# Attention through packed queries with a maxout layer: projection 1 moved to other PSUM banks, and a new order of the steady list

## The chip, the cores and the metric

One core of a Trainium2 chip. The metric is the device time of one execution in microseconds; the kernel is one launch, and the host only lays out inputs and outputs. Several runs are made and their median is told; the profile is of one execution of its own.

## The reference

Eight batches of eight heads, 576 positions and 64 numbers a head; 32 packed queries `p` per head; then a layer with 512 inputs, 768 hidden units and 512 outputs. All in fp32.

```python
p_packed = sm_attn(p, k, v)              # 32 packed queries attend over 576 keys
out = sm_attn(q, p_packed, p_packed)     # 576 queries attend over the 32 packed rows
x = out.transpose(0, 2, 1, 3).reshape(B * S, H * D)
h = np.maximum(np.maximum(x @ w1, x @ w2), x @ w3)
return h @ w_out
```

## The kernel before, in words

The second attention and the first layer are joined: `project` (line 444) computes p_packed @ w for each of six tiles j of 128 hidden units, all three weight matrices at once, and the layer is then the attention weights times that product. Each fp32 operand of a large product is split into a high and a low part, and three matmuls stand for one.

Work goes by batch, and each batch has steps with a letter: S scores of the packed queries (`scores`, line 263), A their maximum and exponential (`weigh`, line 281), X the turning of the exponentials, two transposes on DVE and then 16 small copies issued on SyncE (`spread`, line 325), V the packed values (`values`, line 344), K their turn into `pt_sb`, Q the second scores (`queries`, line 376), B the second softmax (`attend`, line 394), P the projection, N the first layer of one tile (`layer_in_fast`, line 535, from batch 2 on), E the maximum over its products (`maximum_fast`, line 579), H splits and differences of the hidden units (`halves`), T differences of the attention weights, O the output layer (`layer_out_fast`, line 771) and F its end with the stores. Small k, v, q and w are loads on SyncE's queue.

The order is written out by hand, in three lists of words: START (batches 0 and 1 and the weights), LOOP (run for batches 2 to 6) and LAST (batch 7). In a word the letter is the step, the first digit the batch, counted from the loop's own, and the next ones the tile, group or half; v, g or a at the end put it on DVE, POOL or ACT. Each time a word comes up, that step's generator goes on to its next `yield`. So N05 is the next piece of tile 5 of this batch, and P11 the next piece of projection 1 of the next batch; v11 loads v of group 1 of the next batch. On each engine and on SyncE's queue instructions stand in the order of the words. A word for a batch beyond the last is passed over.

In the loop PE works through tiles 0 to 5 of batch b and its output layer, and between them the small steps of batch b+1: scores, values, queries and projections 0 to 2. Projections 3 to 5 of a batch come in its own turn. The small steps use a part of the TensorE array (64*32 or 128*32 in the profile), the tiles and the output layer the whole (128*128).

PSUM has two pools: `ps_big` (two buffers of two banks: scores, values, queries, projections 0, 1, 2 and 5) and `ps_moe` (four banks: the sums of tiles and output layer, and projections 3 and 4). Where a projection lies in `ps_moe`, its r = 0 and r = 1 are two tiles, and each is read by instructions of its own; in `ps_big` one instruction reads both. The readers are ACT (`pf` line 469, `ph` line 475) and DVE (`pl` line 477). A tile's sums are e, x, u, y and f, a bank each; DVE's joins (line 587) and ACT's copies read them. In SBUF the pool with tag "b" has eight buffers, shared by the loads of k, q and v, the two sides of the 16 copies, and the hidden units.

`values` takes its matmuls so that groups 0 and 1 alternate: two matmuls read v of group 0, the next two of group 1. The last 16 of 80 read the small part of v that the second DMA of `load_v` (line 181) brings.

Of the kernel before, what the change touches and what calls it, by code (L numbers as in the profile page):

```python
# [64 lines left out]
E100 B21 E101 C65 W0a E111 E100 P12 N11 C62 C62 C63 C63 P13 C62 P12 W0v H03a C64 N05 C63 E101 N05 P13 E051a  # L65
C63 P12 B21 C62 N05 E111 B20 P15 E051 E051 C64 W0g P14 P15 P15 N13 N13 B21g B21 H02g H03v H03v N12 C64 E120a
N12 E120 E130a E130 N13 N15 N13 N13 E130 R0v H05a N15 N13 H03v N15 N15 N12 N12 C64 W2v N15 W1v W2v E131a E131
N12 N12 E150a E150 N15 E131 E150 H10v B21 W1g W2g W0a W0g W2a W2v E151a W1g E151 E121a W1a E120 W1v W2a H05v
H05g P14 H05g O0 O0 E121 E121 P14 E151 H03a W2g W1a W1v N14 N14 H01a F0 F0 H03v N14 N14 N14 W1v N14 W2v R3v
R1v P21 O0 E140a O0 W2v W1a E141a B21a F0 H05a H11g R2g B21 E140 E140 E141 E141 H01v H14v H12v B20v H12a H05v  # L70
O0 F0 F0 O0 O0 O0 H12g O0 B20 B20 B20a F0 W1v H11v H10a H10v H11v H11g W2v O0 B20 F0 F0 H13a k31 P21 P21 P21
F0 P21g F0 O0 B20g B20 O0 O0 O0 B21v B21 F0 B20a P22 F0 P21v F0 P20 F0 F0 F0 H14a H14g B21a H13v H13v P21v
H15a P20 H13v O1 O1 O1 O1 H15v H15v O1 H11a H11v P21a H13a H15v F1 F1 F1 P22 P22 H13v k30 P21v H15a H15v O1 O1
O1 O1 O1 B20v O1 O1 F1 F1 F1 P20 F1 O1 T2g T2v B21v T2v O1 T2g F1 F1 T2a P20 P20g F1 R5v F1 F1 P22 F1 F1 F1
# [825 lines left out]
```

## Time and profile before

| | us |
|---|---|
| median of 3 runs (457.0 to 457.44) | 457.03 |
| the profiled execution, its own time | 456.87 |
| its span, first to last instruction | 454.8 |
| PE busy | 448.5 |
| VectorE (DVE) busy | 389.0 |
| GpSimd (POOL) busy | 266.7 |
| ScalarE (ACT) busy | 253.7 |

The span is what the profile shows; the time of an execution holds some 2 us more around it. PE's busy time is a union of matmuls whose ends are modelled, so two starts are the safer measure of what a matmul costs. An engine's idle time counts only where PE waits for it.

### The profile page before, as it was taken

The page shows a single profiled execution, that of the slowest core. Times are in us where ns is not written, and L with a number is a line of the kernel's source. Part 1 is how long each engine was busy: PE and PEld are TensorE (multiplying, and loading weights), DVE is VectorE, ACT ScalarE, POOL GpSimd, SP SyncE. Part 2 cuts the span into 40 slices and gives each one's busy share as a digit, 9 for nine tenths or more (in the row PEclk, how much of TensorE's full clock was granted, in tenths as well). Part 3 has the DMA queues.
Part 4 walks back from the last instruction along what each step waited for, and adds up shares of the span by engine and source line. Part 5 has one row for each costly group of instructions (what it writes and reads, how often), then busy time and mean ns, then how long its engine had stood idle before and what let it go on. Part 6 is the DMA issues. An engine that isn't in the chain of part 4 may idle for free.

```text
span 454.8 us, 11856 instructions
## 1 busy us (share of the span) xinstructions
PE 448.5 (99%) x4616; PEld 391.0 (86%) x4616; DVE 389.0 (86%) x825; ACT 253.7 (56%) x552; POOL 266.7 (59%) x280
## 2 busy tenths in 40 slices
...
GB/s 315 398 386 370 330 66 275 2 0 1 140 109 169 111 178 1 61 208 90 128 0 134 161 144 48 27 203 81 175 1 79 192 95 4 1 105 1 1 2 104
DMA packets 35783, 55.68 MB, mean 122 GB/s; under 512 B 17296, under 2 KB 26512, under 8 KB 35728
## 3 DMA queue, kind: packets, MB, share of 16 engines
...
q14 instruction: 19, 0.16, 0.1%
...
## 4 chain that ended last, share of the span: by engine, by line
PE 82%; DMA 12%; SPq 3%; DVE 1%; ACT 1%; issue 1%; POOL 0%; POOLq 0%; DVEq 0%; ACTq 0%
PE mo L784 22%; PE mx L543 10%; PE me L543 9%; PE mo L707 7%; DMA wi<-in_wi 7%; PE mu L543 6%; PE pw L459 6%; PE mf L543 6%; PE mi L630 6%; PE my L543 3%; DMA q<-in_qt 3%; SPq L339 2%; DMA v<-in_va 2%; PE s L386 2%; PE av L357 2%; PE s L273 1%
## 5 line engine op out<-in xcount | busy, mean ns | idle before, releaser
L672 POOL TENSOR_TENSOR r<-r 128x288 f32<-128x288 f32 (+1 forms) x39 | 45.4, 1164 | 59.1 <-DVE r L672 22.9
L477 DVE SCALAR_TENSOR_TENSOR pl<-pw,ph 128x768 fp32r<-128x768 f32 (+1 forms) x61 | 46.7, 775 | 11.4 <-ACT ph L475 11.2
L486 POOL TENSOR_TENSOR pf<-pf 128x128 f32<-128x128 f32 x72 | 40.7, 576 | 10.1 <-ACT pf L469 6.8
L153 POOL TENSOR_TENSOR sl<-pf,sh 128x384 fp32r<-128x384 f32 x28 | 30.6, 1100 | 27.2 <-DVE sh L150 17.7
L630 PE MATMUL mi<-a2h,ph 128*128 128x288 f32 x144 | 44.1, 306 | 0.0
L630 PE MATMUL mi<-a2l,ph 128*128 128x288 f32 x144 | 42.5, 295 | 0.0
L630 PE MATMUL mi<-a2h,pl 128*128 128x288 f32 x144 | 42.4, 294 | 0.0
L475 ACT ACTIVATE ph<-pw 128x768 fp32r<-128x768 f32 (+1 forms) x61 | 40.0, 680 | 2.8 <-PE pw L459 1.9
L459 PE MATMUL pw<-w_sb,pt 64*32 64x384 f32 x768 | 39.1, 490 | 0.1
L469 ACT ACTIVATE pf<-pw 128x512 f32<-128x512 f32 (+1 forms) x48 | 22.3, 492 | 26.4 <-PE pw L459 26.3
L225 POOL TENSOR_TENSOR w_sb<-w_sb,wi 128x512 int32<-128x512 int32 x18 | 23.7, 1327 | 21.7 <-DVE w_sb L221 16.2
L543 PE MATMUL me<-a2h,ph 128*128 128x288 f32 x108 | 32.6, 302 | 0.0
L630 PEld LDWEIGHTS mi<-a2h,ph 128*128 128x128 f32 x144 | 27.0, 188 | 6.4 <-issue 3.0
L784 PE MATMUL mo<-ych,xh 128*128 128x288 f32 x108 | 32.1, 298 | 0.0
L784 PE MATMUL mo<-ych,xl 128*128 128x288 f32 x108 | 31.9, 295 | 0.0
L543 PE MATMUL me<-a2h,pl 128*128 128x288 f32 x108 | 31.8, 294 | 0.0
L543 PE MATMUL me<-a2l,ph 128*128 128x288 f32 x108 | 31.8, 294 | 0.0
L784 PE MATMUL mo<-ycl,xh 128*128 128x288 f32 x108 | 31.8, 294 | 0.0
L148 ACT COPY r<-me 128x288 f32<-128x288 f32 x35 | 14.2, 405 | 25.1 <-PE me L543 25.1
L630 PEld LDWEIGHTS mi<-a2l,ph 128*128 128x128 f32 x144 | 27.0, 188 | 0.1
L630 PEld LDWEIGHTS mi<-a2h,pl 128*128 128x128 f32 x144 | 27.0, 188 | 0.0
L648 DVE TENSOR_TENSOR r<-mi,r 128x288 f32<-128x288 f32 x48 | 20.6, 447 | 3.1 <-PE mi L630 2.0
...
## 6 DMA issues: line engine op xcount, KB each, us to landing
...
q<-in_qt SPq DMA_DIRECT2D x16, 576.0 KB, 6.2
wi<-in_wi SPq DMA_DIRECT2D x18, 512.0 KB, 8.4
v<-in_va SPq DMA_DIRECT2D x16, 512.0 KB, 7.3
wi<-in_wo SPq DMA_DIRECT2D x6, 512.0 KB, 6.0
...
```

Source lines behind the costliest of these rows:

```text
L153: on(default).tensor_tensor(out=lo, in0=src, in1=hi.bitcast(F32), op=ALU.subtract)
L225: nc.gpsimd.tensor_tensor(out=dst.bitcast(I32), in0=dst.bitcast(I32), in1=up, op=ALU.add)
L459: nc.tensor.matmul(out=ps[r][NP * n:NP * n + NP, 0:NW * P], lhsT=pt_sb[b % 2][o, NP * n:NP * n + NP], rhs=w_sb[o, j, n * NW * P:(n + 1) * ...
L469: nc.scalar.activation(out=f[:, r], in_=x[:, :, 0:2 * P], func=AF.Copy, scale=2.0 ** -WS)
L475: nc.scalar.activation(out=hi[:, r], in_=x, func=AF.Copy, scale=2.0 ** -WS)
L477: nc.vector.scalar_tensor_tensor(out=lo[:, r], in0=x, scalar=2.0 ** -WS, in1=hi[:, r].bitcast(F32), op0=ALU.mult, op1=ALU.subtract,)
L486: on("g").tensor_tensor(out=f[:, k], in0=f[:, x], in1=f[:, y], op=op)
L543: nc.tensor.matmul(out=ps[:, 0:HS], lhsT=w[wi], rhs=x[xi], start=first and n == 0, stop=n == 2, skip_group_check=not first,)
L630: nc.tensor.matmul(out=sums[b, j, hf, x][:, 0:HS], lhsT=w[:, r, x * P:(x + 1) * P], rhs=a[:, c], start=(r == 0 and n == 0), stop=(r == R - ...
L672: less = lambda out, x, y: on("g").tensor_tensor(out=out, in0=x, in1=y, op=ALU.subtract)
L707: nc.tensor.matmul(out=ps[:, 0:HS], lhsT=w[:, x, m * P:(m + 1) * P], rhs=h[:, z], start=(p == 0 and i == 0), stop=(p == NQ - 1 and i == 2),)
L784: nc.tensor.matmul(out=ps[:, 0:HS], lhsT=w[:, x, m * P:(m + 1) * P], rhs=h[:, z], start=(not onto and p == 0 and i == 0), stop=(p == NQ - ...
```

## The change

Projection 1 joins 3 and 4 in `ps_moe` from batch 2 on, with two tiles and two sets of reads. The list LOOP is written anew, START from the end of its twelfth line, and LAST too. In LOOP, PE's order changes in these places: scores stand ahead of tile 0 instead of behind its first product; the two projections 3 and 5 come after tile 0 instead of after tile 1; queries come one product later; and projections 0, 2 and 1 stand together ahead of the last two products of tile 5, where 0 and 2 stood behind its first product and 1 behind its last. SyncE's order in LOOP was v11, q11, v10, the copies X1, q10, k20, k21; it is now q11, k20, v10, the copies X1, v11, q10, k21. In START behind the copies it was w64, w65, q21, q20, w62, w63, k31, k30; it is now w62, w65, w64, q20, w63, q21, k30, k31. Many small steps change engine or place. The lines below are LOOP in full, the first changed lines of START, the last of LAST, and the function.

```diff
 START = """
 ...
-C51 P04 E031a N04 N04 N04 P05 E031 B11 v20 B11a E040v E040 B10 H01a H01v N04 N04 N04 E021 w61 C61 E031 P05
-E041a P05 N05 N05 N05 E040 w60 C60 B10g B10g B11g H00a N10 C61 E041 P11 Z20 E050a H00v X2 C60 C60 E041 C61
-E050 P11 V201 Z21 V201 N11 N11 K2 w64 N10 C61 E110v E110 E050 H01g H01g w65 C65 C65 N11 q21 N11 N10 K2a E100v
-N10 H04v H04a q20 Q2 N11 w62 N10 E111a E110 C60 W0v N10 W0v W0v W0a w63 W0g H02v H02a E101a C65 P13 H04v B20
+C51 P04 E031a N04 N04 N04 P05 E031 B11 v20 B11a E040v E040 B10 H01a H01v N04 N04 N04 E021 w61 E031 H00a H00g
+Z20 P05 w60 C60 P05 N05 E041a E041 N05 E041 C61 C61 B10g B10v H01v P11 B11g N10 E050a H02v E040 H04g N10 N10
+C60 X2 Z21 H04a H02a V201 P11 N05 C60 H04v E100a C61 C61 E100 C60 E050 E050 w62 C62 N05 N05 E051a E051 N10 N10
+w65 C65 E101a W0v W0g W0g R1v N11 w64 q20 V201 K2 K2a C65 C65 N11 N11 E110a E101 N11 w63 H03a H02v E110 E110
+C65 H03v E100 W0a q21 C63 Q2 B20 B21 N11 N11 E111v E111 E111 W0g W0a C63 C63 P13 P15 C64 P13 P13 H03v C64 N10
 ...
 LOOP = """
-N00 S1 A11 N00 N00 N00 A10 E00a E00a E00a N00 N00 E00 E00a E00 N00 N00 N00 v11 E00 E00 E00 A10 Z10 E00 A11 A11
-X1 X1 N01 N01 N01 E01a E01a N01 N01 N01 E01a E01 E01a N01 N01 q11 E01 E01 E01 E01 N01 E01 H01v H00g H00g H00g
-P03 P03 P03 P03 P03 P03 P03 P05 v10 N02 H01v H01g N02 N02 N02 P05 E02a E02a N02 E02a N02 N02 P03v E02 E02a
-H01g N03 N02 N02 E02 E02 P03g P03v P03a P03g N03 N03 Z11 E02 E02 E02 E03a E03a H02v N03 N03 E03a N03 H01g E03
-E03a N03 N03 E03 P05 X1 P05 E03 P04 H02g H02g V101 P04 N03 P04 P04 P04 q10 V101 P04 P04 K1 K1v N04 E04a N04
-P05g E03 E03 E03 P04g P05g P04g Q1 P04g k20 E04a N04 B10 E04a P04g P04g H03a N04 N04 H01g N04 N04 V101 B10
-B10g E04 E04a N05 E05a N04 N04 P10 B11 E04 A10 E04 P05v P12 N05 N05 E04 E04 B10 B10 P05g P10 E04 P05g P05 B11
-P10 N05 P10 P10g E05a N05 E05a E05 E05a N05 E05 H04g H04a N05 E05 N05 N05 B11g H03v P11 H04v O0 O0 P12 P12 B11
-O0 P10g E05 E05 F0 H03v E05 B11 O0 B10a B10 B10v H05a B11a H05v P11 P11 H03g P05 P05 F0 F0 k21 H03a H05v O0 F0
-P12 B10 H03v O0 O0 H05g H05a B11 F0 P10g P11 H05v F0 O0 O0 O0 B11g B11 P10a P11g B10a B10g T1g F0 F0 F0 O0
-B11a F0 P12g B11v F0 O0 P12v O0 F0 P12g T1g T1v T1v P11v P11v P10v O0 T1a T1v P11v P11g P11 P12a F0 T1a T1v F0
-P12g P12 P10 P10 P11 P11 P10 P12 P12
+S1 A11 q11 k20 A10 N00 N00 N00 E00a v10 E00a E00v A10 N00 E00 N00 N00 X1 E00a E00 N00 E00 N00 N00 A11 P03 P05
+P03 P03 X1 E00 E00 N01 E00 P03 P03 P03 P03 P03g P03v H00g H00v N01 N01 N01 H00g E01a E01a E01v N01 E01 N01 X1
+E01a N01 N01 N01 E01 N02 N02 N02 E01 P05 E01 E01 E01 E02a E02a A11 Z10 P03g E02a N02 N02 N02 N02 H01g E02 E02a
+N02 E02 E02 P05 E02 E02 H01g H01g v11 N03 E03v P03a N02 E02 N03 N03 P03g E03a E03a N03 N03 H01g N03 N03 P05
+E03 E03a P05v P05g E03 N03 P04 V101 P05v H02v E03 E03 E03 Z11 N03 P05g P04 P04 P04 P04 P04 P04 V101 V101 N04
+P04g P04g K1 H02a N04 N04 K1a P04g P04a q10 H02v E04v E04a E03 Q1 P05g B10 B10 P04g N04 E04a H01a E04 N04 N04
+N04 E04a E04 N04 N04 N05 E05a E04 H01g N05 N05 N05 E04 E05a E05a H03a A10 N05 N05 N05 E04 E04 B11 B10g B10
+H04g H04g E05 P10 P12 B11 E05a P11 N05 H04v B11g P11 P12 P11 P11 P05 P12 E05 E05 N05 E05 B10 B10a O0 O0 O0 O0
+E05 E05 F0 P11 B10 P11 P12 P11 P12v H05a H03g H03g H05v P10 H03v B11 F0 F0 H05g F0 B11 B11a B11 O0 O0 O0 H03a
+P11g B10v B10 k21 F0 P10 F0 P11v P11g H03v O0 H05g H05a H05v O0 O0 P05 P12g P12g F0 F0 P05 F0 P10 P10g B10a
+B10g B11g F0 B11 B11a P12a P10g O0 O0 T1g F0 O0 P10v P10g T1v F0 B11v T1v P11a T1v T1a T1v P10v T1a T1g P10
+P11g F0 P10 O0 P10 F0 P12g P12 P12 P12
 """
 ...
 LAST = """
 ...
-E04 N04 H02a E04 E04 E04 P05g P05a N05 N05 P05g N05 N05 E05v E05v E05a E05 N05 N05 E05v H04g H04a H04v N05 E05
-E05 H03a N05 E05 H02g O0 N05 E05 E05 H05a O0 O0 O0 F0 F0 F0 H05v H05v H01g H01v F0 H03g O0 H03g P05 H03v H01v
-H03a H03v H05v H05v F0 O0 O0 P05 P05 F0 F0 O0 H05v O0 F0 F0 O0 F0 O0 O0 F0 O0 F0 F0 O0 F0
+P05a E04 E04 E04 E04 H02a N04 E04 P05g P05 H04v N05 E05a H02v N05 N05 N05 E05a N05 E05a N05 N05 E05 E05a N05
+N05 H04g E05 E05 E05 E05 E05 H05v H05v H03g H04g H05v H03v O0 O0 O0 H01g H01a H05v H03g F0 F0 F0 O0 F0 O0 F0
+O0 F0 H03v H03g H01v P05 P05 H03v H05a H05v O0 O0 F0 F0 O0 F0 O0 F0 O0 O0 F0 O0 F0 O0 F0 F0
 """
 ...
     def project(b, j):
 
         parts = [slice(0, R)]
-        if j == 0 and b == 0 or j in (3, 4) and b >= 2:
+        if j == 0 and b == 0 or j in (1, 3, 4) and b >= 2:
 
             parts = [slice(r, r + 1) for r in range(R)]
             ps = [ps_moe.tile([P, 512], F32, name=f"pw{b}_{j}_{r}", tag="moe") for r in range(R)]
 ...
```

## Rows read from the trace of the kernel before

**Rows 1.** The page of the profile, busy time of each engine (share of the span) and its instructions.

```profile
PE 448.5 (99%) x4616; PEld 391.0 (86%) x4616; DVE 389.0 (86%) x825; ACT 253.7 (56%) x552; POOL 266.7 (59%) x280
```

**Rows 2.** Busy time by windows, one steady batch: the stretch, its length and, for each engine, busy us and instructions; then the granted clock of TensorE as a share of full speed, DMA share and GB/s.

```profile
246.80:299.80 53.00, 53.00 (x567) 47.02 (x567) 47.11 (x100) 29.77 (x68) 33.69 (x37) 1.00 0.35 104
```

**Rows 3.** The timeline of PE around the projections 0 and 2 of the next batch, which are one block (start in us, us from the first start to the last end, engine, line, operation, out<-in, tile, count).

```profile
276.21 0.29 PE L543 MATMUL mf<-a2h,pl 128*128 128x288 f32 x1
276.34 0.29 PE L543 MATMUL mf<-a2l,ph 128*128 128x288 f32 x1
276.56 1.52 PE L459 MATMUL pw<-w_sb,pt 64*32 64x384 f32 x32
278.01 0.40 PE L543 MATMUL mx<-a2h,ph 128*128 128x288 f32 x1
278.25 0.29 PE L543 MATMUL mx<-a2h,pl 128*128 128x288 f32 x1
```

**Rows 4.** The timeline of PE around projection 1 of the next batch, between tile 5 and the output layer; the same columns.

```profile
281.57 0.29 PE L543 MATMUL mf<-a2l,ph 128*128 128x288 f32 x1
281.80 0.88 PE L459 MATMUL pw<-w_sb,pt 64*32 64x384 f32 x16
282.60 0.40 PE L784 MATMUL mo<-yah,xh 128*128 128x288 f32 x1
282.84 0.30 PE L784 MATMUL mo<-yah,xl 128*128 128x288 f32 x1
```

**Rows 5.** The timeline of PE in the same batch: its first matmul, scores, values and queries of the next batch.

```profile
246.62 0.29 PE L543 MATMUL me<-a2h,ph 128*128 128x288 f32 x1
...
247.51 0.47 PE L273 MATMUL s<-kt 64*32 64x288 f32 x8
...
267.46 1.46 PE L357 MATMUL av<-v,xt 128*32 128x64 f32 x80
...
271.15 0.47 PE L386 MATMUL s<-q,pt 64*32 64x288 f32 x8
```

**Rows 6.** The timeline of SyncE's queue in that batch (start, us from the first issue to the end of the last, line, tile, count of DMAs).

```profile
247.73 0.41 SPq L184 DMA_DIRECT2D v<-in_va  x1
...
248.81 0.53 SPq L193 DMA_DIRECT2D q<-in_qt  x1
249.43 0.38 SPq L184 DMA_DIRECT2D v<-in_va  x1
...
254.73 10.87 SPq L339 DMA_DIRECT2D xt<-x  x16
265.70 0.54 SPq L193 DMA_DIRECT2D q<-in_qt  x1
```

**Rows 7.** The DMA issues of two narrow windows that hold the first v load of a batch (195.0 to 195.5 and 247.5 to 248.15): count, KB each, us from issue to landing.

```profile
v<-in_va SPq DMA_DIRECT2D x1, 512.0 KB, 3.9
...
v<-in_va SPq DMA_DIRECT2D x1, 512.0 KB, 4.5
```

**Rows 8.** The same view of windows that hold the q load behind the 16 copies: 159.5 to 161, 213.25 to 214 and 265.65 to 267 (318.5 to 320 and 371.8 to 373 have the row of the third again).

```profile
q<-in_qt SPq DMA_DIRECT2D x1, 576.0 KB, 5.7
...
q<-in_qt SPq DMA_DIRECT2D x1, 576.0 KB, 3.6
...
q<-in_qt SPq DMA_DIRECT2D x1, 576.0 KB, 4.2
```

**Rows 9.** The timeline of DVE at the start of that batch: maximum and negated scaled maximum, then joins of tile 0, then the two transposes that SyncE copies (in brackets the idle time before, and what ended it).

```profile
248.87 0.76 DVE L286 TENSOR_REDUCE mx<-s 128x1 f32<-128x576 f32 x1 [0.62 <-PE s L273]
...
250.52 0.15 DVE L287 TENSOR_SCALAR nm<-mx 128x1 f32<-128x1 f32 x1
250.60 0.46 DVE L587 TENSOR_TENSOR r<-my,r 128x288 f32<-128x288 f32 x1
250.97 0.45 DVE L587 TENSOR_TENSOR r<-me,r 128x288 f32<-128x288 f32 x1
...
253.24 1.43 DVE L333 STREAM_TRANSPOSE x<-a 128x576 f32<-128x576 f32 x2
```

**Rows 10.** The timeline of ACT there: the exponential of r = 0.

```profile
250.83 0.75 ACT L291 ACTIVATE a<-s,nm 128x576 f32<-128x576 f32 x1
```

**Rows 11.** The timeline of PE in the first list: the places where it is idle between 66 and 76 us.

```profile
67.21 1.44 PE L357 MATMUL av<-v,xt 128*32 128x64 f32 x74 [0.15 <-DMA xt<-x]
...
75.55 0.72 PE L386 MATMUL s<-q,pt 64*32 64x288 f32 x16 [1.03 <-DMA q<-in_qt]
```

**Rows 12.** The timeline of SyncE's queue there.

```profile
65.94 1.01 SPq L172 DMA_DIRECT2D wi<-in_wo  x2
68.68 1.31 SPq L193 DMA_DIRECT2D q<-in_qt  x2
70.04 2.03 SPq L172 DMA_DIRECT2D wi<-in_wo  x2
```

**Rows 13.** Groups of instructions by line and shape, 194 us to the end, DVE (count, busy us, mean ns of one, idle before).

```profile
L477 DVE SCALAR_TENSOR_TENSOR pl<-pw,ph 128x768 fp32r<-128x768 f32 x17 | 15.9, 938 | 3.5 <-ACT ph L475 3.5
...
L477 DVE SCALAR_TENSOR_TENSOR pl<-pw,ph 128x384 fp32r<-128x384 f32 x20 | 10.5, 552 | 5.8 <-ACT ph L475 5.8
```

**Rows 14.** The timeline of DVE around the end of tile 5 in that batch: a wide split, and the reading of tile 5's x.

```profile
281.15 0.75 DVE L153 TENSOR_TENSOR ybl<-r,ybh 128x576 fp32r<-128x576 f32 x1
...
282.85 0.45 DVE L587 TENSOR_TENSOR r<-mx,r 128x288 f32<-128x288 f32 x1
```

More of the change, by code (lines that the diff above doesn't have):

```diff
@@ L65 @@
[L65 to L74, printed above, removed]
@@ L75 @@
-P20v P20v P20a T2v T2a P21 T2g P22g P22g P22g P22g P22g P20v P20 P22 P20 R4g P20 F1
+C51 P04 E031a N04 N04 N04 P05 E031 B11 v20 B11a E040v E040 B10 H01a H01v N04 N04 N04 E021 w61 E031 H00a H00g
+Z20 P05 w60 C60 P05 N05 E041a E041 N05 E041 C61 C61 B10g B10v H01v P11 B11g N10 E050a H02v E040 H04g N10 N10
+C60 X2 Z21 H04a H02a V201 P11 N05 C60 H04v E100a C61 C61 E100 C60 E050 E050 w62 C62 N05 N05 E051a E051 N10 N10
+w65 C65 E101a W0v W0g W0g R1v N11 w64 q20 V201 K2 K2a C65 C65 N11 N11 E110a E101 N11 w63 H03a H02v E110 E110
@@ new lines @@
+C65 H03v E100 W0a q21 C63 Q2 B20 B21 N11 N11 E111v E111 E111 W0g W0a C63 C63 P13 P15 C64 P13 P13 H03v C64 N10
+C62 C62 N05 C64 P15 W0g P15 N13 N13 N13 H01v P12 W0g W0a C62 B21 P14 C63 E130a E051 P12 B21g N13 N13 N15 N15
+E150a E101 E130 H01a P12 N12 W1g k30 C64 H10v N12 N12 W2g W2g E131v E131 E120a H03v W1g W1v E130 W2v E120 E120
+W1a E150 N13 E131 H05a N12 N15 N15 W1v H05v H05g W2a W2v W2a H05g W0g E150 P14 P14 N12 N12 E121a E151a O0 N15
+N14 N14 E121 E121 E151 B21 B21 B21v H01g B21 H03a B20 E140a N14 N14 N14 F0 W1a E140 E140 W2v W2v R2g O0 F0 W1v
@@ new lines @@
+O0 O0 E141a B21v H05a B20v B20 H03v H12v W1v F0 F0 H05v W2a H10a W1a W1g N14 E141 E141 N15 E151 H13g O0 F0 O0
+O0 O0 O0 O0 O0 H11a H12a H12v H10v W2v k31 F0 R0v O0 O0 F0 F0 F0 H13v H14g H14a H13g H13v F0 O0 H11v H11g R3g
+P22 P22 B20 B20v P20 B20 H11v F0 F0 F0 F0 H11a F0 F0 H14v B20v B21 H15a O1 O1 H13a H15v H15g H15v O1 O1 F1 P20
+P20 O1 O1 H11v B20 H15a H15v H13v O1 P22 P22 P20 P20g P22g P22g F1 B21a F1 F1 F1 F1 F1 O1 O1 O1 F1 F1 R4g B20a
+B20g T2g T2g P21 B21v T2v T2g T2a T2v O1 F1 F1 P20v P20g P21 P21 P21 P21 P21 P21 P21v P22v F1 F1 O1 O1 F1 P20a
@@ L76 @@
+P20v P20 T2a O1 P21g P21g P21a T2g R5g P22a P22g F1 P21g F1 P20 P20 P22
 """
 LOOP = """
-N00 S1 A11 N00 N00 N00 A10 E00a E00a E00a N00 N00 E00 E00a E00 N00 N00 N00 v11 E00 E00 E00 A10 Z10 E00 A11 A11
-X1 X1 N01 N01 N01 E01a E01a N01 N01 N01 E01a E01 E01a N01 N01 q11 E01 E01 E01 E01 N01 E01 H01v H00g H00g H00g
-P03 P03 P03 P03 P03 P03 P03 P05 v10 N02 H01v H01g N02 N02 N02 P05 E02a E02a N02 E02a N02 N02 P03v E02 E02a
-H01g N03 N02 N02 E02 E02 P03g P03v P03a P03g N03 N03 Z11 E02 E02 E02 E03a E03a H02v N03 N03 E03a N03 H01g E03
@@ L98 @@
-N02 N02 N02 E02a N02 N02 P03g P03v P03g E02a N02 N03 E02 E02a N02 E02 E02 E02 E02 N03 E03a E03a P03g P03g N03
-N03 E03a E03 N03 N03 E03v E03 N03 N03 E03 H01g E03 H01v E03 P04 P04 P04 P05 P04 P04 P04 P04 P04g P05 P05 N02
-E02 P04g N03 P04g E03 N04 N04 H02v P04a P04v E04a E04a P05 P05v N04 N04 P05g N04 N04 E04a N04 E04 E04a N04 E04
-E04 N04 H02a E04 E04 E04 P05g P05a N05 N05 P05g N05 N05 E05v E05v E05a E05 N05 N05 E05v H04g H04a H04v N05 E05
-E05 H03a N05 E05 H02g O0 N05 E05 E05 H05a O0 O0 O0 F0 F0 F0 H05v H05v H01g H01v F0 H03g O0 H03g P05 H03v H01v
@@ L103 @@
-H03a H03v H05v H05v F0 O0 O0 P05 P05 F0 F0 O0 H05v O0 F0 F0 O0 F0 O0 O0 F0 O0 F0 F0 O0 F0
+N00 E00v N00 E00v N00 E00a N00 E00 N00 E00a N00 E00 N00 N00 E00 E00 E00 N01 N01 N01 E01a E01a N01 N01 N01 E01a
+N01 E01 E01a E01 E01 E01 N01 P03 N01 N00 E01 E01 N02 N02 P03 P03 P03 P03 N02 P03 P03 E00 H00v E02a E02a H00a
+N02 P03g P03g P03g P03a H01a P03g E02v E02 N02 E02v N02 E02 N02 N03 N02 E02 N03 E03a E03a N03 E03a E02 E02 N03
+N03 E03 N03 N03 E03a E03 N03 P04 P04 P04 P04 H01g H00g H01g E03 E03 E03 P04 P04 P05 P04 P04g P04g N02 E02 P05
```

3 lines of the change are left out of this document (1 added, 2 removed).

## The prediction

> **What bounds the kernel now.** The page's engine line comes first: PE is busy 448.5 of 454.8 us [rows 1]. One steady batch by windows says the same from nearer: PE busy through all 53.0 us, DVE 47.1, ACT 29.8, POOL 33.7, granted clock 1.00 [rows 2]. So in the loop nothing is gained by faster DVE, ACT or POOL work; time comes only from PE's own list, or is lost when something PE needs comes late. PE's timeline then shows where its list holds more than matmul time: where it passes from full 128*128 matmuls to the small 64*32 ones (p_packed @ w, scores, queries) and back [rows 3, 4]. Last, SyncE's list beside it [rows 5, 6], because the change reorders the loads, and the last load before the values stage is what can be late.
>
> The sum is made against the profiled execution: span 454.8 us, its own time 456.87, so 2.1 us lie around the span; the median of the runs is 457.03, 0.16 above it. I add the difference to 457.0. A measurement of this kernel can tell about 0.2% (0.9 us) from no change.
>
> **1. One block fewer.** Before, projections 0 and 2 of the next batch are one block, and 1 a block of its own between tile 5 and the output layer. The pair: last full matmul starts 276.34, the second full one after it 278.25 [rows 3], 1.91 us for 32 small matmuls. Alone: 281.57 to 282.84 [rows 4], 1.27 us for 16. Two full steps of 0.13 (276.21 to 276.34 [rows 3]) would be there anyway, in both: that leaves 1.65 and 1.01. Sixteen more in an open block therefore cost 1.65 - 1.01 = 0.64, sixteen alone 1.01, and joining saves 1.01 - 0.64 = **0.37 us a batch**. The loop runs for five batches and each projects for the next, so **-1.85 us**. The third projection's banks are other banks, but pair and solo hold the same 16 matmuls, so I give it the pair's rate; bounds are 0.64 to 1.01 for it, that is 0 to -1.85. Count of the other blocks: the same in the loop (scores only moves ahead of tile 0), in the first list and in the last.
>
> **2. Projection 1 split by r.** Its wide reads of PSUM become two narrow ones each. On DVE that is pl, 2 x 552 instead of 938 ns [rows 13], +0.17 us; for pf and ph on ACT I take twice 0.2. ACT idles 23 us a batch and DVE 6 [rows 2], so nothing on the path; if DVE were full, 0.2 x 5 = 1 us.
>
> **3. The loads, where I expect the loss.** SyncE before: v of group 1, q of group 1, v of group 0, then the 16 small xt copies, then q of group 0, then k [rows 6]. After: q1, k0, v0, the 16 copies, **then v1**, then q0, k1. The values block needs v of both groups: its third matmul reads group 1. So v1 now has to land after the copies are issued and before PE comes to values.
>
> When PE comes: values starts 267.46, with the batch's first matmul at 246.62 (I call this B): B+20.84 [rows 5]. The same matmuls and blocks stand ahead of it after, so B+20.84 again.
>
> When the copies start: now 254.73 = B+8.11 [rows 6]. The new list puts scores first and its softmax chain early on DVE, so this moves up. Scores to first maximum is 1.36 us (247.51 to 248.87), both maxima and negations end 1.80 later (250.52 + 0.15) [rows 5, 9]. With scores starting at B+0.09 that is B+3.25. Then exp of r=0 starts 0.16 after the last negation and takes 0.75 [rows 10]: B+4.2. The list then has transpose r=0, two joins, transpose r=1 on DVE: 0.72 (half of 1.43) + 2 x 0.4 (a join starts 0.37 after the one before, 250.60 to 250.97) + 0.72 [rows 9] = B+6.45; exp of r=1 runs on ACT meanwhile. First copy 0.06 later, **B+6.5**, 1.6 us earlier than now. It can't be below about B+6.2, since every link is a dependence or DVE's own order; a DVE still busy with the previous batch makes it B+7.
>
> The copies take 10.87 us to issue [rows 6], so v1 is issued at about B+17.45. Landing: the first v of a batch took 3.9 to 4.5 us [rows 7]; the q that follows the copies directly, a little larger, took 3.6 to 5.7, mostly 4.2 [rows 8]. I take 4.2, as its place in the queue is just the one v1 gets: **B+21.65, 0.8 us after PE is there**. Ends: B+6.2 + 10.8 + 3.6 = B+20.6, no wait; B+7 + 11.1 + 4.5 = B+22.6, 1.8 us. The small second part of v, issued right behind, is read only by the last fifth of the block and hides behind the rest. Five batches: **+4.0 us** (0 to +9). Queued behind the waiting values block on PE stand tile 3's f, tiles 4 and 5, the projections and the output layer, so nothing makes the wait up. v0, now behind q1 and 640 KB of k0, has until B+20.84 like v1 and is issued in the first few microseconds; k0 early costs a buffer, which is why q0 must wait for one.
>
> The trace has 512 KB at 3.9 to 4.5 us [rows 7]. The Trainium skill, "DMA: Bandwidth & Descriptors", section "Anatomy of one DMA — SWDGE (gpsimd) path", fits one transfer as 2.0 us plus its bytes over 436 GB/s, which as an estimate from that page is 3.2 us; by it the sum would be that of the rival "short landing" below. The rows of v disagree with it, by 0.7 us at least.
>
> q0, now behind v1 and waiting for the buffer that the copies read, lands some 6 us after the copies' issue, about B+23.5; queries are due 3.69 after values (271.15) [rows 5] and two products later in the new list, B+24.9. Covered by 1.4 us, more if values waits. The k loads have half a batch.
>
> **4. Banks of the layers' sums.** Projection 1 now takes two of the four banks while tile 5 still holds e, x and u, then tile 5's f takes one, so the output layer's first step waits for DVE's reading of tile 5's x. Before, that reading ran 282.85 to 283.30, 0.7 us after the output layer's first matmul [rows 4, 14], and that layer now starts 1.0 us earlier against it; against this stands that the two wide splits ahead of it (from 281.15, 1.3 us) [rows 14] become one reduction of 0.7. Ends 0 and 1.1 us a batch. By the order of DVE's list the reading ends about as PE arrives; I take 0.1: **+0.5 us**.
>
> **5. The first list.** PE's one real idle time is 1.03 us at 75.55, for batch 2's q, and 0.15 at 67.21 [rows 11]. Now q1, q0 are issued at 68.68 and the last two w loads behind them [rows 12]; after, three w loads precede q0 and the fourth precedes q1, but one layer step of 0.8 us more stands before values and about two more between values and queries. q1 is then issued where the last w is now, by 72.07 at the latest [rows 12], and with the 5.56 us from the end of the q issues (69.99) to PE's going on (75.55) it is there by 77.6; PE comes to queries at 75.55 - 1.18 + 3 x 0.8 = 76.8. That is a wait of 0.8 at most if the issues don't stretch, and none if the third w, which finds the queue empty at 67, pulls the rest forward. I take 0.5 instead of 1.18: **-0.6 us** (-1.2 to +1). The rest of the first list and the last list keep their matmuls and blocks: nothing, ± 0.5.
>
> **Sum:** -1.85 + 4.0 + 0.5 - 0.6 = +2.05, so 457.0 + 2.05 = **459.0 us**. The terms' bounds make this case's own range 457.4 to 461.5.
>
> **Rivals.**
> *In time (faster).* v1 lands before PE reaches values because the copies start sooner than I read them. Then -1.85 - 0.6 + 0.25 = -2.2: 454.8. It decides at a copies' start of about B+5.75 with 4.2 us to landing. For it: the chain's links are read from another order. Against: each is a dependence. Chance 0.20.
> *Short landing (faster).* v1 alone in the queue lands faster than the q behind the copies: the best q, 3.6 us for 576 KB [rows 8], scaled to 512 KB is 3.2, so B+6.5 + 10.9 + 3.2 = B+20.6 and again 454.8. Against: no first v was under 3.9 [rows 7]. Chance 0.07. The Trainium skill's fit named above, of the page "DMA: Bandwidth & Descriptors", is this case.
> *Even.* A wait near 0.35 us a batch eats just the joining: -1.85 + 1.75 + 0.3 - 0.6 = -0.4, 456.6. Chance 0.15.
> *Banks.* The output layer waits 1.1 us in each batch for DVE as well (89% busy [rows 2]), +5 on top: 464. Against: projections 3 and 4 take two such banks today with no gap in PE. Chance 0.08.
> *Forecast:* 0.50.
>
> **Numbers.** Range 454.6 to 461.8: it takes in the forecast's own range and the cases in time, short landing and even, and leaves out the banks and the far ends. Faster 0.30 (in time, short landing, a little of even), same 0.14, slower 0.56.
>
> **What would show it.** Right: PE idle of 0.5 to 1.3 us before each of the five values blocks, released by the landing of v; copies issued from about B+6.5; a three-projection block of 48 matmuls in about 2.1 us. Wrong: no gap there and a batch of 52.5 us; or the copies starting at B+5.5; or gaps before the output layer's first matmul, which are the banks.

## The result: 463.64 us, slower by 1.35%

The changed kernel took 463.64 us (median of five runs, 462.40 to 464.66) against 457.03 for the one before (five runs, 456.90 to 458.64): ratio 1.0135, interval 1.0107 to 1.0163, 6.6 us slower. The forecast was 459.0 and its range ended at 461.8. The profiled execution took 462.40 with a span of 460.3 us, before 456.87 and 454.8: the two traces show 5.5 us of the difference, and the rest lies in runs that left no trace.

The page of after, engine busy times, for [rows 1]: PE has the same 4616 matmuls and is busy 2.7 us more; POOL, with 16 instructions more, 23.6.

```profile
PE 451.2 (98%) x4616; PEld 393.2 (85%) x4616; DVE 392.7 (85%) x820; ACT 253.0 (55%) x559; POOL 290.3 (63%) x296
```

The five batches of the loop by windows (stretch, length, PE busy and instructions, clock, DMA share, GB/s), for [rows 2]; each stretch begins one step of 0.13 us after the last matmul of the batch before:

```profile
144.25:197.46 53.21, 53.08 (x567) 1.00 0.37 115
197.46:250.69 53.23, 53.11 (x567) 1.00 0.34 104
250.69:304.34 53.65, 53.15 (x567) 1.00 0.33 103
304.34:357.67 53.33, 53.10 (x567) 1.00 0.34 104
357.67:410.98 53.31, 53.21 (x567) 1.00 0.26 79
```

Cut at the same matmuls, the difference stands so. The first list (up to batch 2's first matmul) ends at 144.25 instead of 140.75: **+3.5 us**. The five batches take 266.7 instead of 264.6: **+2.1**. Batch 7 takes 49.3 instead of 49.4. So more than half of the traced loss came from the first list, for which the prediction had expected a gain of 0.6.

**The loop.** SyncE's queue of the third of these batches, for [rows 6], and PE at values, for [rows 5]:

```profile
253.47 0.47 SPq L184 DMA_DIRECT2D v<-in_va  x1
...
257.12 11.48 SPq L339 DMA_DIRECT2D xt<-x  x16
268.70 0.53 SPq L184 DMA_DIRECT2D v<-in_va  x1
```

```profile
271.54 0.31 PE L357 MATMUL av<-v,xt 128*32 128x64 f32 x4
272.31 1.54 PE L357 MATMUL av<-v,xt 128*32 128x64 f32 x76 [0.47 <-DMA v<-in_va]
```

Values starts at B+20.85, B being 250.69, and stops for v1. The wait was foretold; its place was the third matmul, the first to read group 1, and the trace puts it behind the fourth. From 271.54 to the end of the 80, 2.31 us pass instead of 1.46: 0.85 lost. The five batches lose 0.48, 0.47, 0.85, 0.58 and 0.35, 2.73 in all, each some 0.2 more than v1 lands behind PE's arrival. The landing of v1, for [rows 7, 8] (DMA issues of the windows 268.5 to 269.2 and 214.8 to 215.25; the other three show 3.5 to 3.8):

```profile
v<-in_va SPq DMA_DIRECT2D x1, 512.0 KB, 3.5
...
v<-in_va SPq DMA_DIRECT2D x1, 512.0 KB, 3.7
```

PE around the joined block, for [rows 3, 4], and in tile 5 just ahead of it, where gaps had not been foretold; then DVE's joins and POOL's work at that time, for [rows 14]:

```profile
281.56 0.29 PE L543 MATMUL mx<-a2l,ph 128*128 128x288 f32 x1
281.89 0.40 PE L543 MATMUL mu<-th,ph 128*128 128x288 f32 x1
...
282.45 0.40 PE L543 MATMUL my<-a2h,sh 128*128 128x288 f32 x1
...
282.82 0.29 PE L543 MATMUL my<-a2l,sh 128*128 128x288 f32 x1
...
284.01 0.29 PE L543 MATMUL mu<-tl,ph 128*128 128x288 f32 x1
284.24 2.17 PE L459 MATMUL pw<-w_sb,pt 64*32 64x384 f32 x48
286.33 0.40 PE L543 MATMUL mx<-th,sh 128*128 128x288 f32 x1
286.57 0.29 PE L543 MATMUL mx<-th,sl 128*128 128x288 f32 x1
```

```profile
279.72 0.45 DVE L587 TENSOR_TENSOR u<-mu,u 128x288 f32<-128x288 f32 x1
280.20 1.27 DVE L587 TENSOR_TENSOR r<-u,r 128x288 f32<-128x288 f32 x1
281.39 0.45 DVE L587 TENSOR_TENSOR r<-mx,r 128x288 f32<-128x288 f32 x1
```

```profile
279.98 1.17 POOL L415 TENSOR_TENSOR e<-e,m 128x576 f32<-128x576 f32 x1
```

The block: 284.01 to 286.57 is 2.56 us; less the two full steps of 0.13, that is 2.30 for 48 matmuls, where pair and solo took 1.65 + 1.01. That is -0.36 a batch, the foretold gain. In tile 5, six steps from 281.56 to 282.82 take 1.26 instead of 0.79. The chain reads backwards: u waits for a bank that the join r<-mx,r frees; that join stands behind r<-u,r; and r<-u,r, whose two operands both lie in SBUF, took 1.27 instead of some 0.5 while POOL's subtraction from 279.98 to 281.15 was at work. Over the loop such gaps between full matmuls hold 3.7 us, before 2.0 (steps longer than 0.16 us count, without the first behind a block of small matmuls). Loop: +2.7 (v) +1.65 (tile 5) -1.85 (joining) -0.5 (small waits for q that are gone) = +2.0, against 2.1 measured.

**The first list.** PE's waits of the whole span that lie there, for [rows 11] (who waited, for whom, us, times, longest), and DVE and POOL around batch 1's output layer:

```profile
PE pw L459 <- POOL w_sb L225: 1.1, 1, 1.1
PE s L386 <- DMA q<-in_qt: 1.0, 1, 1.0
PE mo L707 <- DVE ycl L153: 0.6, 1, 0.6
...
PE mo L707 <- DVE yal L153: 0.3, 1, 0.3
```

```profile
122.20 1.87 DVE L672 TENSOR_TENSOR r<-r 128x576 f32<-128x576 f32 x1
124.00 0.81 DVE L730 SCALAR_TENSOR_TENSOR s<-mo,v 128x288 f32<-128x288 f32 x2
124.73 0.81 DVE L730 SCALAR_TENSOR_TENSOR u<-mo,u 128x288 f32<-128x288 f32 x2
125.46 0.74 DVE L153 TENSOR_TENSOR yal<-r,yah 128x576 fp32r<-128x576 f32 x1
```

```profile
122.03 1.43 POOL L755 TENSOR_TENSOR t<-v,t 128x576 f32<-128x576 f32 x1
```

By starts of matmuls the 3.5 us are: an early w load at 21 us, +0.85; the queries' wait for q, +0.54 beyond what it was; values and the turn of K, -0.1 together; gaps in batch 1's output layer at 126, 134 and 136 us, +0.53, +0.86 and +0.37, with some 0.3 of smaller ones. The first of these is chance: up to there the lists are the same word for word, and the wait was 0 to 1.1 us in the kernels below without pattern, 0 in `best` and 1.1 in `best_again`, which are one kernel. The gaps are the change's: no kernel with the old first list has them, every one with the new has 1.2 us or more of them. As in tile 5, a DVE step of two SBUF operands (1.87 instead of 0.75) overlaps POOL's, and what PE needs stands behind it.

### The profile page after: what moved, and what is told of

Same layout as the page of the kernel before. It is cut to its first block, busy times and chain, and to the rows that moved or that the text cites. A ratio compares the mean times of both kernels' runs of the same rounds, so it can differ in the third digit from the quotient of the medians.

```text
span 460.3 us, 11868 instructions
## 1 busy us (share of the span) xinstructions
PE 451.2 (98%) x4616; PEld 393.2 (85%) x4616; DVE 392.7 (85%) x820; ACT 253.0 (55%) x559; POOL 290.3 (63%) x296
## 4 chain that ended last, share of the span: by engine, by line
PE 87%; DMA 6%; DVE 5%; issue 1%; ACT 0%; SPq 0%; DVEq 0%
PE mo L784 22%; PE mi L630 12%; PE me L543 9%; PE mx L543 9%; PE pw L459 7%; PE mf L543 6%; PE mu L543 6%; PE mo L707 4%; PE my L543 3%; DMA q<-in_qt 3%; DMA wi<-in_wi 2%; PE av L357 2%; PE s L273 2%; PE s L386 2%; PE idle L162 1%; DMA v<-in_va 1%
## 5 line engine op out<-in xcount | busy, mean ns | idle before, releaser
L486 POOL TENSOR_TENSOR pf<-pf 128x128 f32<-128x128 f32 x73 | 40.8, 569 | 32.0 <-ACT pf L469 23.6
L672 POOL TENSOR_TENSOR r<-r 128x288 f32<-128x288 f32 (+1 forms) x46 | 49.3, 1079 | 14.5 <-DVE r L587 6.6
L477 DVE SCALAR_TENSOR_TENSOR pl<-pw,ph 128x384 fp32r<-128x384 f32 (+1 forms) x67 | 46.6, 719 | 4.1 <-ACT ph L475 3.8
L475 ACT ACTIVATE ph<-pw 128x384 fp32r<-128x384 f32 (+1 forms) x67 | 40.4, 638 | 7.7 <-PE pw L459 7.3
L469 ACT ACTIVATE pf<-pw 128x256 f32<-128x256 f32 (+1 forms) x54 | 22.2, 457 | 40.1 <-PE pw L459 40.1
L148 ACT COPY r<-me 128x288 f32<-128x288 f32 x25 | 10.0, 400 | 30.9 <-PE me L543 30.4
L543 PEld LDWEIGHTS me<-a2h,ph 128*128 128x128 f32 x108 | 20.3, 188 | 5.4 <-DVE r L587 3.1
```

What stands on the lines that cost most here:

```text
L469: nc.scalar.activation(out=f[:, r], in_=x[:, :, 0:2 * P], func=AF.Copy, scale=2.0 ** -WS)
L475: nc.scalar.activation(out=hi[:, r], in_=x, func=AF.Copy, scale=2.0 ** -WS)
L477: nc.vector.scalar_tensor_tensor(out=lo[:, r], in0=x, scalar=2.0 ** -WS, in1=hi[:, r].bitcast(F32), op0=ALU.mult, op1=ALU.subtract,)
L486: on("g").tensor_tensor(out=f[:, k], in0=f[:, x], in1=f[:, y], op=op)
L543: nc.tensor.matmul(out=ps[:, 0:HS], lhsT=w[wi], rhs=x[xi], start=first and n == 0, stop=n == 2, skip_group_check=not first,)
L672: less = lambda out, x, y: on("g").tensor_tensor(out=out, in0=x, in1=y, op=ALU.subtract)
```

## The experiments

**Theory**: the loss has two independent sources, v1 behind the copies (in the loop; the waits in tile 5 follow from it) and the new first list; the joined block gains 1.85 us. **Rivals**: the joining gains nothing; the tile 5 waits are the banks' own; the first list matters only by handing the loop another state. "First list" below is the time of batch 2's first matmul in the profiled execution, "loop" the length of the five batches. Both are of one execution each: the same kernel gave 141.04 and 144.18 for the first list (`best`, `best_again`) and 261.7 and 261.8 for the loop, so a first list of one trace can be 3 us off by chance.

| kernel | us, median | range | ratio to before, same chip | first list | loop |
|---|---|---|---|---|---|
| before | 457.03 | | | 140.75 | 264.6 |
| changed | 463.64 | 462.4 to 464.7 | 1.0135 [1.0107, 1.0163] | 144.25 | 266.7 |
| start_old | 459.68 | 459.2 to 460.2 | 1.0047 [1.0029, 1.0066] | 141.89 | 267.1 |
| start_new | 459.44 | 458.8 to 460.5 | 1.0038 [1.0019, 1.0057] | 142.99 | 264.9 |
| last_old | 463.32 | 463.2 to 463.7 | 1.0129 [1.0115, 1.0144] | 143.55 | 268.3 |
| loads_old | 457.87 | 455.6 to 458.8 | 1.0004 [0.9989, 1.0020] | 145.00 | 261.6 |
| v1_first | 459.14 | 456.4 to 460.5 | 1.0027 [1.0007, 1.0047] | 143.81 | 262.6 |
| sub_dve | 460.74 | 460.4 to 462.2 | 1.0081 [1.0058, 1.0104] | 143.18 | 266.2 |
| best | 454.77 | 454.1 to 456.0 | 0.9946 [0.9928, 0.9964] | 141.04 | 261.7 |
| best_again | 454.88 | 454.3 to 457.2 | 0.9953 [0.9934, 0.9971] | 144.18 | 261.8 |
| solo | 457.06 | 455.6 to 458.8 | 0.9993 [0.9977, 1.0009] | 141.14 | 263.4 |
| h14_early | 458.57 | 456.4 to 460.7 | 1.0023 [1.0001, 1.0044] | 143.63 | 261.7 |
| r_pool | 458.25 | 456.6 to 460.6 | 1.0005 [0.9988, 1.0021] | 144.06 | 262.6 |
| q_first | 456.61 | 455.7 to 459.3 | 0.9981 [0.9964, 0.9997] | 142.12 | 264.1 |
| f0_first | 458.06 | 456.0 to 460.3 | 1.0009 [0.9990, 1.0029] | 142.20 | 262.8 |
| best_q | 457.52 | 455.0 to 459.9 | 0.9991 [0.9973, 1.0009] | 143.87 | 263.9 |
| best_q2 | 456.67 | 454.3 to 458.5 | 0.9985 [0.9970, 1.0000] | 141.00 | 262.2 |

### The halves: start_old, start_new, last_old

`start_old` is the changed kernel with the lines of START of before; projection 1 of batch 2, which that list projects, stays in `ps_big`. `start_new` is the reverse: the kernel before with START of the changed one, and projection 1 of batch 2 alone in `ps_moe`. `last_old` is the changed kernel with LAST of before (its eight lines exchanged). The diff is the condition of `start_old`.

```diff
-        if j == 0 and b == 0 or j in (1, 3, 4) and b >= 2:
+        if j == 0 and b == 0 or j in (3, 4) and b >= 2 or j == 1 and b > 2:
```

> The first list as it was (projection 1 of batch 2 in its old banks), the steady and the last list as changed. Theory (the time went in three places: the first list +3.5 us, waits for v1 +2.7, waits of tile 5 +1.8, against joining -1.85): 463.6 - 3.4 = 460.2, batch 2 starting near 140.8 us instead of 144.3. Rival (the loop alone makes the loss, the first list only shifts where PE waits): 463.6, no change.

> The reverse: the first list as changed, with projection 1 of batch 2 in the layers' banks, the steady and last list as before and projection 1 of later batches in its old banks. Theory: 457.0 + 3.4 = 460.4, with the gaps at batch 1's output layer (2 us) seen again. Rival: 457.0 to 457.5, the first list costs nothing by itself.

> The changed kernel with the old last list, so that the first list and the loop are new and the last is old. Theory (the two halves add and the last list does nothing: 49.30 us of span against 49.41 before): the time is 457.4 + 2.0 + 2.3 = 461.7, between 461 and 462.5, with the last batch within 0.2 us of 49.4. Rival 1 (the last list costs 2 us by some wait that its span hides): 459.5 to 460.5, below the sum of the halves. Rival 2 (the halves cost more together, the last list nothing): 463 or more, as the whole change.

The first list alone costs 2.0 us, loop and last list 2.3 (medians beside the kernel before on the same chip), so the first list is a source of its own, and `start_new` keeps the old loop (264.9). The last list does nothing that shows: without it 463.3. But the halves measured alone add up to 4.3 and together they cost 5.8 to 6.6; that 1.5 to 2.3 us is **not explained** here. In the traced executions the spans do add within what chance moves, +3.6 and +2.8 against +5.5 (changed) and +6.7 (`last_old`). A part that varies is the wait for v: 2.6 us over the loop in `start_old`, 2.7 in the changed kernel, 4.2 in `last_old`, as the copies' issue takes 10.7 to 11.5 us and v1's landing 3.5 to 4.1.

### The loads of the loop: loads_old, v1_first

Only the places of the load words in LOOP change (the lines below are parts of lines, cut at `...`).

```diff
-S1 A11 q11 k20 A10 N00 N00 N00 E00a v10
+S1 A11 v11 q11 A10 N00 N00 N00 E00a v10
 ...
-v11 N03 E03v P03a
+q10 N03 E03v P03a
 ...
-P04a q10 H02v
+P04a k20 H02v
```

> The changed kernel with SyncE's loads of the steady list in their old order (v1, q1, v0, the 16 copies, q0, k0, k1), nothing else. Theory: the wait of 0.35 to 0.85 us ahead of each values block goes, -2.7 in all: 460.9; values blocks of 1.39 us again. Rival (PE would wait there anyway, for the copies or for other work just behind): 463.0 or more, as the same time turns up later in the batch.

```diff
-S1 A11 q11 k20 A10 N00 N00 N00 E00a v10 E00a
+S1 A11 q11 k20 A10 N00 N00 N00 E00a v10 v11 E00a
 ...
-H01g H01g v11 N03
+H01g H01g N03
```

> The changed kernel with one load moved: v of group 1 ahead of the 16 copies, right behind v of group 0; k of group 0 stays early and q of group 0 late. Theory (v of group 1 behind the copies makes both the wait ahead of the values and, through later softmaxes, the waits in tile 5): both go, 2.7 and 1.6 us over the loop, 463.6 - 4.3 = 459.3, near the 457.9 of the kernel with all loads in the old order. Rival (the waits in tile 5 come from the new order of the small steps, or q of group 0 behind the copies holds queries up): only the wait ahead of the values goes, 461, or another one takes its place, 462 or more.

`loads_old` wins back 5.8 us, twice what the wait for v was worth: the loop falls to 261.6, 3.0 under before, with neither a wait for v nor the long gaps in tile 5, though banks, words and engines there are those of the changed kernel. `v1_first` moves one load and gets the loop to 262.6: 4.1 of the 5.1 us. The rest is its third batch, where PE waits 0.3 for q0, which still stands behind the copies, and then in tile 5. So the late v1 is the cause of both waits, and k0's early place does no harm that shows. With late values, and so late queries, the second softmax's subtraction on POOL falls onto the join in tile 5.

Single batches bear this out. 261.6 is the loop at its best: the same LOOP with the same loads took 261.6 to 264.1 in the nine traces below that have it, since now and then a batch waits for the copies or for q. In six batches of `v1_first`, `r_pool`, `q_first` (two), `f0_first` and `best_q` PE lost 0.2 to 1.3 us at values or queries, and these have the wait at tile 5's u. No batch that lost less there has it. One that lost 1.05 at queries (`best_q`, the first) has not, so how late matters too.

### The join in tile 5: sub_dve

```diff
-N05 N05 N05 E04 E04 B11 B10g B10
+N05 N05 N05 E04 E04 B11 B10v B10
```

> The changed kernel with one word moved from POOL to DVE, the subtraction of the maximum in the second softmax for r = 0 in the steady list. Theory: that subtraction on POOL holds up DVE's join of two SBUF tiles (1.27 us instead of 0.5) and so the reading of tile 4's x, whose bank tile 5's u waits for; without it the join takes 0.5 us, the gap of 0.3 to 0.5 us at tile 5 goes: 463.6 - 1.8 = 461.8. Rival (DVE at 89% is simply too full, and 0.8 us more a batch makes it later): 463.6 to 466.

The subtraction e<-e,m of the second softmax goes from POOL to DVE. DVE in tile 5:

```profile
278.56 0.45 DVE L587 TENSOR_TENSOR u<-mu,u 128x288 f32<-128x288 f32 x1
279.05 0.46 DVE L587 TENSOR_TENSOR r<-u,r 128x288 f32<-128x288 f32 x1
279.42 0.45 DVE L587 TENSOR_TENSOR r<-mx,r 128x288 f32<-128x288 f32 x1
```

The join takes 0.46 instead of 1.27 and the gaps in the loop fall from 3.7 to 1.35 us: POOL's step had been holding it. But the wait for v rose from 2.7 to 3.8, and each joined block took some 2.43 instead of 2.30, 0.65 in five, so the loop gained only 0.6. The whole gained 2.9, part of it in the first list, where nothing was changed.

### The version without the two losses: best, best_again, solo

`best`: START of before (with the condition of `start_old`), LOOP of the change with the loads as in `loads_old`, LAST of the change.

> The old first list, the new loop list with the old order of the loads, the new last list. Theory (first list and late v of group 1 are the two losses, the joined block the one gain, and they add): the first list ends as before, batch 2 starting at 140.8 to 141.9 us, the five batches of the loop take 261.6 as with the old loads alone, the last 49.3: span 451.7 to 452.8, time 453.8 to 454.9, under the kernel before by 2.5 to 3.6 us. Rival (the loop gained with the old loads only because the new first list hands it another state of the queues and buffers): the loop goes back to 264 or more and the time is 456.5 or more.

> The kernel 'best' as it was, beside the one with the old last list. Theory (its gain is the joined block and the loads in their old order, none of it chance): 454 to 455.5, a ratio of 0.992 to 0.997. Rival (the first six runs caught the early part of the first list at its quickest, as the scatter of 'best_q' and 'best_q2' suggests): 456 to 457.

```profile
193.63:245.92 52.29, 52.29 (x567) 1.00 0.35 106
245.92:298.21 52.29, 52.29 (x567) 1.00 0.35 106
```

PE has no idle time in the last four of the five batches (two shown, windows as above), 52.29 us against 53.0 in [rows 2]; the first of the five took 52.59, with a wait of 0.4 in tile 0. The kernel beats the one before and the changed one: 454.8 and 454.9. `solo` takes the joining back:

```diff
-B11 E05a P11 N05 H04v B11g P11 P12 P11 P11 P05 P12 E05 E05 N05 E05
+B11 E05a N05 H04v B11g P11 P12 P11 P11 P05 P12 E05 E05 N05 P11 E05
```

> As the kernel 'best', but the 16 matmuls of projection 1 stand one product of tile 5 later, a block of small matmuls of their own again, still in the banks of the layers' sums. Theory (one block fewer is worth 0.37 us a batch): best + 1.85 us, so 455.7 to 456.7, each batch 0.37 longer with no new wait. Rival (the gain of the new loop list is in its other order, not in the joining): within 0.5 us of best.

```profile
278.69 0.29 PE L543 MATMUL mu<-tl,ph 128*128 128x288 f32 x1
278.92 1.52 PE L459 MATMUL pw<-w_sb,pt 64*32 64x384 f32 x32
280.37 0.40 PE L543 MATMUL mx<-th,sh 128*128 128x288 f32 x1
280.60 0.29 PE L543 MATMUL mx<-th,sl 128*128 128x288 f32 x1
280.74 0.29 PE L543 MATMUL mx<-tl,sh 128*128 128x288 f32 x1
280.96 0.88 PE L459 MATMUL pw<-w_sb,pt 64*32 64x384 f32 x16
281.76 0.40 PE L543 MATMUL mf<-a2h,ph 128*128 128x288 f32 x1
282.00 0.29 PE L543 MATMUL mf<-a2h,pl 128*128 128x288 f32 x1
```

Two blocks again, 1.91 + 1.26 us less four steps of 0.13: 2.65 instead of 2.30. The loop is 1.7 us longer, 0.34 a batch; the medians differ by 2.3, in noisier runs. So of the 2.9 us by which the loop of `best` is shorter than before, the joining is 1.7. The rest was not foretold: the gaps between full matmuls fell from 2.0 to 1.2, and 0.5 of waits for q is gone.

### The gaps of the first list: h14_early, r_pool, f0_first

All three have the loads of `loads_old`; `f0_first` also the order of loads in START that `q_first` has. Each changes one word of START or its place. The changed kernel's two yal and two ycl, which the text compares:

```profile
112.94 1.90 DVE L153 TENSOR_TENSOR yal<-r,yah 128x576 fp32r<-128x576 f32 x2
...
131.00 2.84 DVE L153 TENSOR_TENSOR ycl<-r,ych 128x864 fp32r<-128x864 f32 x2
```

```diff
-B20 H11v F0 F0 F0 F0 H11a F0 F0 H14v B20v
+B20 H14v H11v F0 F0 F0 F0 H11a F0 F0 B20v
```

> The changed kernel with the loads of the loop in the old order (457.9 us) and one word of the first list moved: the difference for the last hidden units of batch 1 ahead of the four pieces of batch 0's output on DVE, instead of behind them. Theory (those pieces and the new place of tiles 4 and 5 make the gaps of 2 us in batch 1's output layer): the first gap of some 0.5 us goes, and a part of the two behind it: 456.6 to 457.4, batch 2 starting 0.5 to 1.3 earlier. Rival (DVE is full there, so whatever stands ahead, something else is late): gap for gap the same, 457.9 within 0.3.

```diff
-k31 F0 R0v O0
+k31 F0 R0g O0
```

> The changed kernel with the loop's loads in the old order (457.9 us) and one word of the first list moved from DVE to GpSimd: a difference of the output weights (0.93 us on DVE at 116.6) in the place where GpSimd stands idle for 1.9 us. Theory (DVE, busy without a break from 116 to 137, is behind by its own load, and PE's gaps of 0.5, 0.9 and 0.4 us in batch 1's output layer are that lag): the lag falls by 0.9 us ahead of the first gap, so 0.5 goes whole and the second shrinks: 456.6 to 457.2, output-layer gaps of 0.8 or less instead of 1.8. Rival (the second and third gaps come from the long subtractions after 129 us, held up by GpSimd beside them): only the first gap goes, 457.4; nothing at all if DVE then waits for PE's sums, 457.9.

```diff
-B20 H11v F0 F0 F0 F0 H11a F0 F0 H14v B20v
+B20 F0 F0 F0 F0 H11v H11a F0 F0 H14v B20v
```

> The kernel 'q_first' (456.6 us) with one word of the first list moved: DVE's join of two SBUF operands (1.87 us at 122.2 in the changed kernel, 0.75 elsewhere) behind two joins that read PSUM, instead of ahead of them, so that those two stand beside GpSimd's subtraction of 1.43 us. Theory (GpSimd's work on SBUF holds up a DVE step whose operands are both in SBUF, and that lag is PE's first gap in batch 1's output layer): the join takes 0.75 to 1.3 instead of 1.87, the two PSUM joins keep their 0.4 each, and the gap of 0.5 at 124 goes or halves: 456.0 to 456.3, batch 2 up to 0.5 earlier. Rival (DVE is late by its own amount of work, or by the two long subtractions behind): the join shrinks but the gaps keep their sum, 456.6; or the PSUM joins are held up as well.

None of the three made the kernel faster. DVE of `h14_early`, of `r_pool` and of `f0_first`, then POOL of `f0_first` (lines one higher, LOOP having a line more):

```profile
121.97 1.49 DVE L154 TENSOR_TENSOR yal<-r,yah 128x576 fp32r<-128x576 f32 x1 [0.30 <-PE mo L708]
123.38 0.75 DVE L673 TENSOR_TENSOR r<-r 128x576 f32<-128x576 f32 x1
```

```profile
111.94 3.75 DVE L154 TENSOR_TENSOR yal<-r,yah 128x576 fp32r<-128x576 f32 x2
```

```profile
119.23 0.76 DVE L731 SCALAR_TENSOR_TENSOR s<-mo,v 128x288 f32<-128x288 f32 x2
119.90 1.20 DVE L673 TENSOR_TENSOR r<-r 128x576 f32<-128x576 f32 x1
...
127.21 4.58 DVE L154 TENSOR_TENSOR ycl<-r,ych 128x864 fp32r<-128x864 f32 x2
```

```profile
119.05 1.43 POOL L756 TENSOR_TENSOR t<-v,t 128x576 f32<-128x576 f32 x1
```

Whatever step of two SBUF operands stands beside POOL's work is the one held up. With yal first, yal takes 1.49 and the join behind it 0.75, and the gap of 0.5 moves into the projection block ahead. With 0.93 us of DVE's work given to POOL, two yal beside it take 3.75, where the changed kernel's two take 1.90. With two joins that read PSUM beside POOL, those take 0.76 together, the SBUF join falls from 1.87 to 1.20 and the first gap goes; but then POOL's next steps fall on the two ycl, which take 4.58 instead of 2.84, and PE waits 2.1 us for them. The sum of the gaps does not fall, and in `f0_first` it grows from 2.0 to 2.9. Which step is held follows what stands beside POOL's, so the overlap is shown for the first gap. That DVE has too much work besides was not tested apart from it: in `r_pool` the work taken from DVE came back as longer yal. No order without the overlap was found for the new first list other than the old list.

### The queries' wait in the first list: q_first, best_q, best_q2

```diff
-R1v N11 w64 q20 V201
+R1v N11 q20 w64 V201
 ...
-N11 w63 H03a
+N11 q21 H03a
 ...
-W0a q21 C63
+W0a w63 C63
```

> The changed kernel with the loop's loads in the old order (457.9 us) and, in the first list, each q load of batch 2 one place further ahead: q of group 0 before the third w load instead of behind it, q of group 1 before the fourth. Theory (queries of batch 2 wait for q because it lands behind the w loads): the wait of 1 to 1.5 us ahead of the queries at 77 to 79 us goes, 456.5 to 457.2. Rival (the wait is for the buffer that the copies free or for the stretch of the whole queue, not for the w loads ahead): the wait stays, 457.9; or a tile waits for the late w instead.

`best_q` exchanges w64 and q21 in the old list; `best_q2` makes w64, w65, q21, q20 into q21, w65, q20, w64.

> The kernel 'best' (454.8 us) with q of group 1 of batch 2 ahead of the third w load in the old first list, where two w loads stood ahead of it. Theory (as for q_first): the wait of 1.1 us ahead of the queries at 75.8 goes, and 453.7 to 454.0 results. Rival (another wait takes its place, w of tile 4 being late, or the q waits for its buffer): 454.8 or more.

> The kernel 'best' (454.8 us) with both q loads of batch 2 further ahead in the old first list: q, w, q, w where w, w, q, q stood, then the last two w loads as before. Theory (the queries wait for the last q, which lands behind whatever stands ahead of it in the queue): one w load of 512 KB fewer ahead of it, so the wait of 1.1 us ahead of the queries falls to 0 to 0.3 and 453.7 to 454.2 results. Rival (the last q lands late because the w loads behind it share the engines, as in 'best_q', or it waits for its buffer): the wait stays at 1 us or more, 454.8 to 457.

In `q_first` the queries take 1.33 us without a wait, and in `f0_first`, with the same loads, 1.5; the kernels with the new list and its own order take 2.3 to 3.4. So q had landed behind the w loads there. By the ratios 1.1 us are won against `loads_old`, but the intervals overlap, so the gain is not clear of noise. In the old list neither order helped, and both kernels are slower than `best`: `best_q` waited 2.3 us for q, and `best_q2` 0.35 for q and then 1.0 in a tile. `best_again`, with nothing changed, waited 2.25 where `best` waited 1.1. What sets this landing from one execution to the next stays open.

A long wait can cost more than itself. PE of `best_again` behind it, and a window (length, PE busy and instructions, granted clock, DMA share, GB/s). The profile names ACT as what ended the wait, but the second q, issued at 69.9, took 7.4 us to land, to 77.3:

```profile
77.41 1.97 PE L386 MATMUL s<-q,pt 64*32 64x288 f32 x32 [2.25 <-ACT yah L148]
...
79.40:81.00 1.60, 1.60 (x7) 0.50 0.00 0
```

The granted clock, 1.00 up to the wait, is 0.50 there (1.2 GHz, the lower of its two levels): a full step takes 0.24 us instead of 0.13, until 81.1. `best_q` shows the same behind its 2.3 us, and seven of its twelve runs have a mean granted clock of 0.993 to 0.996 where all six of `best` have 0.999 or 1.000. In the trace of `f0_first` the 2.1 us for ycl left the clock at 1.00, but six of its twelve runs have 0.995 or 0.996.

## Why the prediction went wrong in size

1. **One block fewer** (-1.85): right, -0.36 a batch in the trace, and `solo` gives 0.34 back.
2. **The split of projection 1** (nothing): right; `best` has it and no gap from it.
3. **The wait for v1** (+4.0): the mechanism and place were right, in the copies' start (B+6.35 to B+6.65 for B+6.5), the issue (B+17.2 to B+18.0 for B+17.45) and PE's arrival (B+20.8 to B+20.95 for B+20.84). The landing was mis-sized: 3.5 to 3.8 us instead of 4.2, so the wait is 2.7 instead of 4.0 in this profile. The q behind the copies, 64 KB larger, was a poor stand-in. The Trainium skill, "DMA: Bandwidth & Descriptors", section "Anatomy of one DMA — SWDGE (gpsimd) path", gave 3.2 as an estimate, by a fit for DMAs issued by GpSimd, while these are issued on SyncE's queue; the trace lies between, 0.3 to 0.6 above it.
4. **Banks** (+0.5, at the output layer): that wait did not come. Another wait for a bank did, 1.65, in tile 5's u and y. The number of banks did not make it: `loads_old` and `best` have the same banks and no such wait. The step that failed is the one that gave the late v no price beyond its own wait: late values push the second softmax, and with it POOL's subtraction, onto a DVE join that frees a bank.
5. **The first list** (-0.6, the rest "nothing, ± 0.5"): this is the step that took the forecast out of its range. Only PE's matmuls and blocks were counted, and they are the same; the steps of DVE and POOL between them are not. In the trace it cost 3.5, of this +1.76 in the output layer, +0.54 for q where -0.68 was reckoned (written as -0.6), and +0.85 that is chance. By experiment it cost 2.0.

That the loop came out near its forecast, +2.1 for +2.65, is in part luck: the wait for v was 1.3 less, the other wait 1.15 more, and 0.5 of waits for q went. The range was also narrower than its own terms: they run from -1.85 to 0, 0 to +9, 0 to +5.5 and -1.2 to +1, which is 454 to 472.5 and not 457.4 to 461.5. And the traces hold 5.5 of the 6.6 us; the rest stays open, as does why the two halves of the change cost less apart.

Of the rivals, the one named banks gave 464, near the 463.64 measured, but by 1.1 us at the output layer in each batch, which no trace shows: that nearness is luck.
